# Moving the last columns' scores and values, and beginning the up matmuls with half contractions, in a fused pooling-attention and gated feed-forward kernel

One Trainium2 chip, one core. The metric is device time in microseconds (us); lower is better. The kernel before takes 303.98 us (median of 3 runs, 303.52 to 304.59).

## The reference

Keys and values of 8 batches x 8 heads (576 tokens, 64 per head) are averaged over groups of 8 tokens, then plain attention, then a feed-forward block with the gate h cos(h):

```python
k_p = k.reshape(B, H, Sp, 8, D).mean(axis=3)          # Sp = 72
v_p = v.reshape(B, H, Sp, 8, D).mean(axis=3)
attn = softmax(q @ k_p^T / sqrt(D))
x = (attn @ v_p).transpose(0, 2, 1, 3).reshape(4608, 512)
h = x @ w_in                                          # 512 -> 2048
out = (h * np.cos(h)) @ w_out                         # 2048 -> 512
```

## The kernel before

The feed-forward runs over nine tiles of 512 tokens (loop variable t). A batch has 576 tokens, so batch b begins 64 b tokens behind tile b. While the down matmuls of tile t run, a list `fill` slips the attention of batch b = t + 1 in among them; each entry is (number of the down matmul ahead of which it is issued, what). A batch is cut into units: u0, u1 (columns 0 to 255, heads 0-3 and 4-7), u2, u3 (columns 256 to 511), and REST (the last 64 columns, all heads). REST of batch t is left for pass t. "Vn" is the values unit of un.

```python
SEG = ((0, 256), (256, 256), (512, 64))
REST = (SEG[2], (0, H))
BY_TOKENS = [(SEG[s], (4 * j, 4)) for s in range(2) for j in range(2)]
...
banks = [psum.tile([128, 2, 512], FP32, name=f"bank{i}") for i in range(3)]
obanks = [psum.tile([128, 512], FP32, name=f"obank{i}") for i in range(2)]
...
def values(b, u, pair, later=None):            # matmuls, 2 logarithms + 1 exponential (ScalarE) ...
    ...
    def mul():                                 # ... and 2 multiplications (VectorE) that write xT
        for hp in range(2):
            nc.vector.tensor_mul(out=x_out(b, u, half[hp]), in0=cols(pair[half[hp], hp, :], u), in1=...)
    if later is None:
        mul()
    else:
        later.append(mul)
...
def up_mm(t, fp, k0=0, k1=KCH):                # a pair of 128-wide chunks; KCH = 4 steps of contraction
    h = banks[fp % 3]
    for j in range(2):
        fc = 2 * fp + j
        for ki in range(k0, k1):               # ki covers heads 2 ki and 2 ki + 1
            nc.tensor.matmul(h[:, j, :], lhsT=w_in_sb[fc // 4][:, ki, ...],
                             rhs=xT[:, ki, t * TILE:(t + 1) * TILE], start=(ki == 0), stop=(ki == KCH - 1))
...
for t in range(NT):
    b = t + 1
    for fp in range(FFCH // 2):                # the up stage: 64 matmuls
        up_mm(t, fp, 2 if t == 0 and fp < 2 else 0)
        ...
        up_g(t, fp, between)                   # cosine (ScalarE), multiplication (VectorE), frees the bank
    ...
    for n, (ms, fc) in enumerate(mms):         # the down stage: 64 matmuls, with fill among them
        while fi < len(fill) and fill[fi][0] <= n:
            fill[fi][1]()
            fi += 1
        down_mm(obanks[ms % 2], ms, fc)
        if fc == FFCH - 1:
            down_out(t, ms, obanks[ms % 2])    # VectorE copies the bank out, then a DMA
```

The softmax here doesn't subtract the row's maximum and nothing guards it: scores larger than these inputs give would overflow.

## Time and profile before

| | before |
|---|---|
| time, us (median of the first 3 runs) | 303.98 |
| span in the profile, us | 302.1 |
| TensorE busy | 97%, full clock |
| one pass, up stage to up stage, t = 1 to 6 | 31.40 to 31.41 us each |

The prediction shows the lines themselves. In them, a row of the order of time has start, length, engine, line, operation, tiles, shapes and count; L297 is an up matmul, L310 a down matmul, L211 scores, L241 values, L252 the multiplication into xT, L316 the copy of a finished down bank, PEld the weight loads. A row of waits has who waited, for what, the total in us, how many times, and the longest; "issue" means that the profile shows nothing that was waited for. Groups overlap at their edges because a matmul is recorded longer (0.38 us) than its slot (0.216 us); so I read starts, not lengths. A gap below is the distance from one matmul's start to the next one's; a hole is what a gap has over its usual value. Pair fp is the pair of 128-wide chunks 2 fp and 2 fp + 1 of the up stage; pair 3 takes the bank that pair 0 has left.

### The profile page before, as it was taken

The numbers are of one execution on the slowest core, as the hardware profiler recorded it, in microseconds if no ns is written. First come the engines' busy times: TensorE is split into PE (matmuls) and PEld (weight loads), VectorE is DVE, ScalarE is ACT, GpSimd is POOL, SyncE is SP. The second block draws the span as 40 slices with busy tenths as digits, with TensorE's granted clock in tenths as the row PEclk, the third lists the DMA queues.
The fourth block names the chain that finished last, engine by engine and source line by source line (L and its number), as shares of the span: only waits on it lengthen the run. The fifth ranks groups of instructions, "written<-read, shape, count | busy, mean of one in ns | idle before, by whom it ended". The sixth has DMA issues, their size and how long they took to land.

```text
span 302.1 us, 4605 instructions
## 1 busy us (share of the span) xinstructions
PE 294.0 (97%) x1798; PEld 141.6 (47%) x1798; DVE 172.3 (57%) x211; ACT 206.8 (68%) x255; POOL 129.8 (43%) x92
## 2 busy tenths in 40 slices
PE   8799999999999999999999999999999999999995
PEld 3545544445544454455444544454444544444444
DVE  5558636574566366645675566656574567425712
ACT  3887897469856986688768876788578956606500
POOL 8553007984973596349733991399100000000000
PEclk9999999999999999999999999999999999999999
DMA  7999999639546943695169617881900330131032
GB/s 152 201 207 206 208 204 196 152 44 174 109 113 105 167 92 70 123 171 113 44 132 161 115 36 162 129 141 36 167 5 1 71 69 0 27 79 35 0 71 71
DMA packets 44006, 32.92 MB, mean 109 GB/s; under 512 B 22096, under 2 KB 39248, under 8 KB 43984
## 3 DMA queue, kind: packets, MB, share of 16 engines
q0 software_dynamic: 19744, 18.07, 38.2%
q1 hardware_dynamic: 24080, 14.42, 21.0%
q8 instruction: 14, 0.23, 0.3%
q10 hardware_dynamic: 160, 0.13, 0.2%
q14 instruction: 8, 0.07, 0.1%
HBM read 36.70 MB, written 9.44 MB: 153 GB/s over the span
## 4 chain that ended last, share of the span: by engine, by line
PE 85%; DMA 10%; POOL 2%; ACT 1%; issue 0%; DVE 0%; POOLq 0%; ACTq 0%
PE obank L310 39%; PE bank L297 37%; DMA w_out_sb<-in_moe_w_out_dram 6%; PE bank L241 5%; DMA w_in_sb<-in_moe_w_in_dram 4%; PE bank L211 3%; PE bank L328 1%; POOL kv_st L84 1%; POOL kp L384 1%; POOL q_b L84 1%; ACT L285 0%; ACT cos L304 0%; ACT ex L218 0%; POOL identity masks.py:197 0%; DVE o_sb L316 0%
## 5 line engine op out<-in xcount | busy, mean ns | idle before, releaser
L310 PE MATMUL obank<-w_out_sb,g_sb 128*128 128x512 bf16 x560 | 132.5, 380 | 0.5 <-DMA w_out_sb<-in_moe_w_out_dram 0.5
L297 PE MATMUL bank<-xT,w_in_sb 128*128 128x512 bf16 x576 | 126.5, 379 | 0.0
L304 ACT ACTIVATE cos<-bank,half_pi 128x1024 f32<-128x1024 f32 x72 | 80.0, 1113 | 63.3 <-PE bank L297 63.3
L307 DVE TENSOR_TENSOR g_sb<-bank,cos 128x1024 bf16<-128x1024 f32 x72 | 88.1, 1225 | 48.2 <-ACT cos L304 48.2
L297 PEld LDWEIGHTS <-w_in_sb 128*128 128x128 bf16 x576 | 55.5, 98 | 68.6 <-DVE xT L252 2.5
L310 PEld LDWEIGHTS <-g_sb 128*128 128x128 bf16 x560 | 52.2, 97 | 56.9 <-issue 3.7
L252 DVE TENSOR_TENSOR xT<-bank,inv 64x512 bf16<-64x512 f32 (+1 forms) x72 | 45.3, 629 | 50.1 <-ACT inv L248 49.2
L141 POOL TENSOR_TENSOR kv_st<-kv_st 72x2048 f32<-72x2048 bf16 x12 | 48.7, 4056 | 35.2 <-DMA kv_st<-in_k_dram 35.2
L247 ACT ACTIVATE lnc<-bank 64x512 f32<-64x512 f32 (+1 forms) x72 | 39.2, 544 | 2.9 <-PE bank L241 1.3
L218 ACT ACTIVATE ex<-bank 72x1024 bf16<-72x1024 f32 (+1 forms) x40 | 35.0, 928 | 5.3 <-PE bank L211 5.2
L316 DVE COPY o_sb<-obank 128x512 f32<-128x512 f32 x35 | 23.6, 689 | 16.8 <-PE obank L310 16.2
L142 POOL TENSOR_TENSOR kv_st<-kv_st 72x1024 f32<-72x1024 f32 x12 | 28.2, 2348 | 1.0
L248 ACT ACTIVATE inv<-lnc 128x512 f32<-128x512 f32 (+1 forms) x36 | 21.0, 583 | 1.1
L241 PE MATMUL bank<-ex,vz 72*128 72x256 bf16 (+1 forms) x176 | 20.0, 243 | 0.2 <-ACT ex L218 0.2
L241 PEld LDWEIGHTS <-vz 72*128 72x128 bf16 x176 | 13.7, 97 | 9.9 <-issue 0.6
L145 POOL TENSOR_TENSOR kp<-kv_st 72x512 bf16<-72x512 f32 x12 | 14.9, 1264 | 0.5
L211 PE MATMUL bank<-qT,kk 64*72 64x256 bf16 (+1 forms) x192 | 13.3, 252 | 1.1 <-ACT qT L193 0.5
L211 PEld LDWEIGHTS <-kk 64*72 64x72 bf16 x192 | 7.6, 110 | 11.9 <-issue 8.1
L285 ACT ACT_TABLE_LOAD x9 | 11.5, 1283 | 0.9 <-PEq L515 0.7
L288 ACT ACT_TABLE_LOAD x9 | 11.5, 1283 | 0.2
L495 POOL COPY gate<-kk 1x1 bf16<-1x1 bf16 x5 | 0.9, 180 | 24.7 <-DMA kk<-kp 24.7
L84 POOL DMA_DIRECT2D q_b<-in_q_dram x10 | 7.7, 773 | 2.7 <-DMA w_in_sb<-in_moe_w_in_dram 1.4
(55 smaller groups left out, 89.8 us busy)
## 6 DMA issues: line engine op xcount, KB each, us to landing
out_dram<-o_sb SPq DMA_DIRECT2D x70, 128.0 KB, 2.4
kv_st<-in_v_dram POOLq DMA_DIRECT2D x8, 576.0 KB, 13.0
kv_st<-in_k_dram POOLq DMA_DIRECT2D x7, 576.0 KB, 7.7
q_b<-in_q_dram POOLq DMA_DIRECT2D x6, 576.0 KB, 9.9
w_in_sb<-in_moe_w_in_dram POOLq DMA_DIRECT2D x4, 512.0 KB, 13.7
w_out_sb<-in_moe_w_out_dram POOLq DMA_DIRECT2D x4, 512.0 KB, 18.4
q_b<-in_q_dram POOLq DMA_DIRECT2D x4, 288.0 KB, 12.1
g_sb<-in_k_dram SPq DMA_DIRECT2D x1, 576.0 KB, 3.5
```

The lines of the kernel that those rows point to most:

```text
L141: add(out=s, in0=x[:, :, 0:4, :], in1=x[:, :, 4:8, :], op=ADD)
L142: add(out=s[:, :, 0:2, :], in0=s[:, :, 0:2, :], in1=s[:, :, 2:4, :], op=ADD)
L211: nc.tensor.matmul(pair[:Sp, bank, c:c + n].rearrange("p (g n) -> p g n", n=64), lhsT=kk[b % 2][half[r], h0 + i, 0:Sp], rhs=att["qT", b][h ...
L218: nc.scalar.activation(out=ex[:, 0:nh * n].rearrange("p (a n) -> p a n", a=2), in_=pair[:Sp, :, 0:nh * n // 2], func=ACTF.Exp, scale=scale ...
L241: nc.tensor.matmul(pair[:, hp, (i // 2) * n:(i // 2 + 1) * n], lhsT=vz[b % 2][:, pj, 2 * hp:2 * hp + 2, :].rearrange("p a d -> p (a d)"), ...
L247: nc.scalar.activation(out=lnc[half[1 - hp]], in_=pair[half[1 - hp], hp, 0:w], func=ACTF.Ln)
L252: nc.vector.tensor_mul(out=x_out(b, u, half[hp]), in0=cols(pair[half[hp], hp, :], u), in1=cols(inv[half[1 - hp]], u))
L297: nc.tensor.matmul(h[:, j, :], lhsT=w_in_sb[fc // 4][:, ki, (fc % 4) * 128:(fc % 4 + 1) * 128], rhs=xT[:, ki, t * TILE:(t + 1) * TILE], st ...
L304: nc.scalar.activation(out=cos, in_=h, func=ACTF.Sin, bias=half_pi[:, :1])
L307: nc.vector.tensor_mul(out=g_sb[:, 2 * fp:2 * fp + 2, :], in0=h, in1=cos)
L310: nc.tensor.matmul(o, lhsT=g_sb[:, fc, ms * 128:(ms + 1) * 128], rhs=w_out_sb[fc // 4][:, fc % 4, :], start=(fc == 0), stop=(fc == FFCH - 1))
L316: nc.vector.tensor_copy(out=o[:, 0:n], in_=ps)
```

## The change

The intent: go to the 64-row mode of the scores once less per pass (REST's scores right behind u2's and u3's); let REST's values come ahead of the last unit V3; and, because V3 is then late, begin the next up stage with matmuls that need heads 0 to 3 alone. V0's multiplication is issued behind the first output copy (list `later`).

```diff
     for t in range(NT):
         b = t + 1
+        if t > 0:
+            up_mm(t, 0, 0, 2)
+            up_mm(t, 1, 0, 2)
         for fp in range(FFCH // 2):
-            up_mm(t, fp, 2 if t == 0 and fp < 2 else 0)
+            up_mm(t, fp, 2 if fp < 2 else 0)
...
-            late = 0 < t and b < B
-            fill = [(1, lambda: scores(t, REST, banks[2])), (12, lambda: values(t, REST, banks[2 if late else 1]))]
+            fill = [(1, lambda: scores(t, REST, banks[2])), (12, lambda: values(t, REST, banks[1]))]
...
-            def two_(n, bank0, bank1):
+            def scores_of(*parts):
                 def go():
-                    for mm in (scores_mm, scores_exp):
-                        mm(b, us[n], banks[bank0])
-                        mm(b, us[n + 1], banks[bank1])
+                    for f in scores_mm, scores_exp:
+                        for b_, u, bank in parts:
+                            f(b_, u, banks[bank])
                 return go
-            fill = [(4, two_(0, 2, 0)), (14, V_(0, 1)), (19, V_(1, 2)), (32, two_(2, 0, 1)), (36, fill[0][1]),
-                    (38, V_(2, 0)), (41, V_(3, 1)), (45, fill[1][1])]
+            fill = [(4, scores_of((b, us[0], 2), (b, us[1], 0))), (14, V_(0, 1, later)), (16, lambda: later.pop()()),
+                    (19, V_(1, 2)), (35, scores_of((b, us[2], 0), (b, us[3], 1), (t, REST, 2))),
+                    (38, V_(2, 0)), (43, lambda: values(t, REST, banks[1])), (46, V_(3, 2))]
```

## The prediction

> **What bounds the kernel now.** I read the page first (busy shares, clock, chain), then the stretches of the main loop, then the waits of TensorE and of its weight loads, and last the order of time in one pass of the loop.
>
> ```profile
> span 302.1 us, 4605 instructions
> PE 294.0 (97%) x1798; PEld 141.6 (47%) x1798; DVE 172.3 (57%) x211; ACT 206.8 (68%) x255; POOL 129.8 (43%) x92
> ...
> PEclk9999999999999999999999999999999999999999
> ...
> PE 85%; DMA 10%; POOL 2%; ACT 1%; issue 0%; DVE 0%; POOLq 0%; ACTq 0%
> ```
>
> TensorE is busy 97% of the span at the full clock, and the chain that ended last is TensorE for 85%. Busy alone does not prove a full TensorE, so I take the pace from starts. In the up stage of the second loop pass, 64 matmuls take 13.81 us on the chain (53.66 to 67.47): 0.2158 us each. That is the pace of a stream without a hole. The stretches from one up stage to the next:
>
> ```profile
> core 0: us, PE busy (x) PEld busy (x) DVE busy (x) ACT busy (x) POOL busy (x), PEclk, DMA share, GB/s
> 53.66:84.98 31.32, 31.32 (x178) 14.87 (x176) 18.33 (x22) 24.14 (x30) 25.81 (x16) 1.00 0.63 115
> 84.98:116.39 31.41, 31.41 (x178) 14.89 (x178) 18.82 (x23) 24.23 (x31) 21.14 (x12) 1.00 0.64 115
> 116.39:147.80 31.41, 31.41 (x178) 14.88 (x178) 18.82 (x23) 24.23 (x31) 19.21 (x12) 1.00 0.64 115
> ```
>
> Each of the six passes t = 1 to 6 takes 31.4 us, alike to 0.1. The 128 large matmuls need 128 x 0.2158 = 27.62; 3.8 us are left for scores, values and what is lost at their edges. Only holes in those edges are to be won. The weight loads show where they are (stretch 60 to 260 us, six passes):
>
> ```profile
> PEld L211 <- issue: 5.5, 13, 0.4
> PEld L211 <- DVE xT L252: 2.5, 6, 0.4
> PEld L297 <- DVE xT L252: 2.5, 6, 0.4
> PEld L310 <- issue: 2.3, 12, 0.2
> ```
>
> Six times a weight load of the up stage (L297) and six times one of the scores (L211) is held by VectorE's write of xT. These idle times are of the weight-load row and lie mostly under the matmul that still runs, so they are not the loss. The loss comes from the starts of TensorE's groups in one pass (start, length, line, count):
>
> ```profile
> 107.27 0.63 PE L211 MATMUL bank<-qT,kk 64*72 64x256 bf16 x8
> 107.83 1.04 PE L310 MATMUL obank<-w_out_sb,g_sb 128*128 128x512 bf16 x4
> 108.80 0.33 PE L211 MATMUL bank<-qT,kk 64*72 64x64 bf16 x8
> 109.06 0.60 PE L310 MATMUL obank<-w_out_sb,g_sb 128*128 128x512 bf16 x2
> ...
> 112.13 4.27 PE L310 MATMUL obank<-w_out_sb,g_sb 128*128 128x512 bf16 x19
> 116.31 0.82 PE L297 MATMUL bank<-xT,w_in_sb 128*128 128x512 bf16 x3
> ```
>
> The last 19 down matmuls take 116.31 - 112.13 = 4.18 us from first start to the first up matmul; at pace they need 4.10. So **the hole ahead of an up stage is 0.08 us**. The group of the last 64 columns (L211, 64x64) sits between down matmuls: from 107.83 to 109.06 are 1.23 us for four down matmuls (0.86) and this group, so it costs 0.37, though its 8 matmuls run in four pairs about 0.033 us apart (0.13, single starts in the trace).
>
> **What the Trainium skill says.** (1) "TensorE: Matmul & The Clock Gate", section "Back-to-back issue gap", gives about 216 ns for 512 columns at full clock as N/2.4 + 2.5, and says that a real stream can sustain 131. This trace agrees with the first (215.8) and not with the second: the pace can't fall below it here. (2) "TensorEngine Tiling (Array Packing)", "Key Properties", says that a change of tiling mode drains TensorE. Scores contract over 64 rows, everything around them over 128 or 72, so each visit is two changes; the trace agrees: four down matmuls ahead of a scores group take 0.97 (107.83 to 108.80) for 0.86, and 0.13 of the 0.26 behind it is not its pairs. (3) The same TensorE page, "Architectural detail: the array is 16× 32×32, not 1× 128×128", has ScalarE and VectorE strictly first in, first out. The trace agrees on VectorE below: an output copy stands between two multiplications that were issued around it. (4) "Perfetto Trace Analysis", "Identifying the Most-Contended Engine", warns that matmul busy is no measure of what is left; that is why I use starts.
>
> **The change, part by part.**
>
> *1. Last columns' scores behind the second score group (six passes).* It removes one visit to the 64-row mode: 0.37 becomes 0.13, which would save 0.24. But it needs bank 2, which the second values unit (V1) has to leave. VectorE and ScalarE in that pass:
>
> ```profile
> 105.19 1.39 DVE L252 TENSOR_TENSOR xT<-bank,inv 64x512 bf16<-64x512 f32 x2 [3.90 <-ACT inv L248]
> 106.61 0.69 DVE L316 COPY o_sb<-obank 128x512 f32<-128x512 f32 x1
> 107.33 1.39 DVE L252 TENSOR_TENSOR xT<-bank,inv 64x512 bf16<-64x512 f32 x2
> ...
> 106.42 0.63 ACT L248 ACTIVATE inv<-lnc 128x512 f32<-128x512 f32 x1
> 107.72 2.41 ACT L218 ACTIVATE ex<-bank 72x1024 bf16<-72x1024 f32 x3 [0.68 <-PE bank L211]
> ```
>
> The change delays V0's multiplication behind the copy, so that the copy runs early (its bank is full at about 103.5) and V1's multiplication starts when its reciprocal is there: 106.42 + 0.63 + 0.03 = 107.08, ends 108.47 instead of 108.72. The joint group starts three down matmuls later than now, at 107.27 + 0.65 = 107.92; its first four pairs, 0.108 apart, end their issue at 108.35. The last columns then want bank 2 and get it at 108.47 + 0.08 = 108.55 (0.08 is what the trace shows from 108.72 to the weight load at 108.80). So **a new hole of 0.20 opens inside the group**. With the 0.26 of the small group the next down matmul (number 35) starts at 108.81 and number 36 at 109.03; today number 36 starts at 109.06. What is left of 0.24 is 0.03.
>
> *2. The exponentials come later.* First exponential: 0.45 behind the group's start (today 107.72 - 107.27), so 108.37 to 109.39 at 1.02. V2 would be issued at 109.03 + 2 x 0.216 = 109.46 and needs it at 109.39 + 0.06 = 109.45: just in time. The third exponential ends near 110.85 (2.41 after 108.37, with slack); the last columns' values, five down matmuls behind V2, come at 109.46 + 0.44 + 1.08 = 110.98: in time. ScalarE is then 0.65 later than today: V2's logarithms and reciprocal, 110.85 to 112.7; the last columns', to 114.0; V3's, to 115.85; table load (1.28) to 117.15. No hole on TensorE from any of them.
>
> *3. V3 last, and half contractions first.* The two half groups need heads 0 to 3 only (V0, V2 and the last columns, written by about 115.1) and banks 0 and 1. The up stage begins near 116.2, so it waits for nothing: **0.08 saved, in the up stages t = 2 to 7**. V3's multiplication runs 115.87 to 117.27 on VectorE; the second halves start 8 x 0.216 = 1.73 after the beginning, 117.95: 0.7 to spare.
>
> *4. The price of halves.* Pair 0 is now complete after 12 matmuls, not 8. Its cosine starts 1.94 after the beginning today (118.25 - 116.31), so 2.80 then; cosine 1.11, multiplication 1.23 and 0.03 between: bank 0 is free at 5.17, seen by TensorE at 5.23. Pair 3 wants it at 24 x 0.216 = 5.18. So **0.04 to 0.05 is lost in every up stage t = 1 to 8**. The kernel has this pattern already at t = 0, where the start of pair 3 is 250 ns behind its predecessor instead of 216: 0.035 measured. I take 0.04.
>
> Sum: 6 x 0.08 (begin) + 6 x 0.03 (scores) - 8 x 0.04 (pair 3) = 0.48 + 0.18 - 0.32 = 0.34 us less. Other engines' work is the same in kind and count. 303.98 - 0.34 = 303.64; I round down to 303.5 because where I chose between two values I took the worse.
>
> **Rivals.** *A: the joint group does not wait for bank 2*, or the wait covers the drain. Then 0.24 instead of 0.03 in six passes, 1.3 us more: about 302.4. For it: dependences may be by part of the bank, so that the first multiplication (0.7 earlier) lets most through. Against: the pairs go to both halves, and today's weight load there does wait for xT. Even then V2 would wait for the first exponential (109.45), which eats most of the gain. *B: the later ScalarE chain becomes the bound*: V3's multiplication is 0.7 later than I have it, or V2 stalls 0.1 to 0.2 on its exponential; six passes of 0.2 give 1.2 us, about 304.8. For it: V2 and the last columns' values have hardly any slack. Against: V3 has 0.7, and a stall at V2 pushes all else back with it. *C: pair 3's wait doubles* (0.09 as at the beginning of an up stage): 8 x 0.05 more, 304.0. *D: DMA or the clock*: nothing in the loop's chain, and the clock is at 9 in all slices; no effect.
>
> **Range and chances.** All terms are hundredths of a us, taken six or eight times; the worst sums that I can build are -2 and +1.5 us. The three runs before spread over 1.1 us. Two per cent are 6.1 us, and all edges of six passes (3.8 us each, most of it needed work) hold nothing like it. Range 302.5 to 304.3; within 2% nearly sure.
>
> **What would show it.** In the changed trace: the pass (up stage to up stage) 31.41 becomes 31.3 to 31.4; the weight load of L297 no longer waits for xT at the beginning; one scores visit less per pass, with 24 matmuls in one group, and inside it a wait of about 0.2 on VectorE's xT; the output copy near 103.6; V2 within 0.05 of its exponential's end; a hole near 0.04 ahead of pair 3. Wrong it would be if the second halves wait for V3's multiplication, if V2 stalls by 0.1 or more, or if the joint group runs through and the pass falls to 31.1.

## The result, and the profile after

303.33 us (median of 4 runs, 303.28 to 303.87) against 303.75 (4 runs of before, 303.52 to 304.59): 0.42 us less. The ratio is 0.9985, 95% interval 0.9962 to 1.0009: same within 2%, and by the times alone not told from no change. (A ratio here is the mean time of one kernel's runs over that of the other's of the same rounds, so not quite the ratio of the medians.) Executions over 1.5% slower than the fastest of the same kernel are left out of the means. The traces are much finer than the times, because the passes repeat. The stretches from up stage to up stage of the kernel after, with the columns as in the prediction:

```profile
core 0: us, PE busy (x) PEld busy (x) DVE busy (x) ACT busy (x) POOL busy (x), PEclk, DMA share, GB/s
53.53:84.83 31.30, 31.30 (x177) 15.07 (x176) 17.25 (x20) 23.38 (x30) 25.76 (x15) 1.00 0.62 115
84.83:116.12 31.29, 31.29 (x177) 15.05 (x176) 18.72 (x23) 24.14 (x31) 19.84 (x12) 1.00 0.63 115
```

A pass is 31.29 to 31.30 us instead of 31.41. What held the weight loads, 60 to 260 us, after:

```profile
PEld L211 <- issue: 5.5, 13, 0.4
PEld L211 <- DVE xT L252: 1.5, 6, 0.2
PEld L310 <- issue: 1.2, 6, 0.2
PEld L297 <- issue: 0.9, 6, 0.2
```

The up stage's wait for xT is gone. L310's edge count halves (12 to 6): one visit to the scores' mode less per pass. Scores still wait for xT, now inside the joint group; and L297 has a new small idle ("issue", 0.9 in six), which is pair 3. TensorE's order of time in the third pass, and VectorE's:

```profile
107.71 0.93 PE L211 MATMUL bank<-qT,kk 64*72 64x256 bf16 x16
108.57 0.82 PE L310 MATMUL obank<-w_out_sb,g_sb 128*128 128x512 bf16 x3
109.23 0.60 PE L241 MATMUL bank<-ex,vz 72*128 72x256 bf16 x4
...
112.07 4.05 PE L310 MATMUL obank<-w_out_sb,g_sb 128*128 128x512 bf16 x18
115.95 1.24 PE L297 MATMUL bank<-xT,w_in_sb 128*128 128x512 bf16 x5
```

```profile
103.27 0.69 DVE L316 COPY o_sb<-obank 128x512 f32<-128x512 f32 x1 [2.20 <-PE obank L310]
104.98 1.39 DVE L252 TENSOR_TENSOR xT<-bank,inv 64x512 bf16<-64x512 f32 x2 [1.01 <-ACT inv L248]
106.87 1.39 DVE L252 TENSOR_TENSOR xT<-bank,inv 64x512 bf16<-64x512 f32 x2 [0.50 <-ACT inv L248]
...
115.63 1.39 DVE L252 TENSOR_TENSOR xT<-bank,inv 64x512 bf16<-64x512 f32 x2 [0.86 <-ACT inv L248]
```

18 down matmuls from 112.07 to the first up matmul at 115.95 take 3.88, which is 18 x 0.2158: no hole. The joint group takes 108.57 - 107.71 = 0.86. V1's multiplication ends at 106.87 + 1.39 = 108.26, inside the group. From the single starts of matmuls in the trace (their gaps, not a duration): ahead of the first REST score the gap is 245 ns where its neighbours have 106, a **hole of 139 ns**; ahead of pair 3 of the up stage it is 249 instead of 216, a **hole of 33 ns**. V3's multiplication ends at 117.02, 1.07 us after the up stage began.

From the first up matmul of pass t = 1 to the start of the last matmul, the trace of before has 244.57 us and that of after 243.93: 0.64 us less in the loop. The part ahead of it has unchanged code; it ends at 53.50 us before and 53.36 after, and anywhere from 53.28 to 53.80 in nine of the ten traces. From the last matmul's start to the end of the span, before has 4.03 us and after 4.21: 0.19 more. Together this makes the 0.6 by which the spans differ; the medians differ by 0.42.

### The profile page after: what moved, and what is told of

Read it like the earlier page. It is cut to its first block, busy times and chain, and to the rows that moved or that the text cites. A ratio compares the mean times of both kernels' runs of the same rounds, so it can differ in the third digit from the quotient of the medians.

```text
span 301.5 us, 4599 instructions
## 1 busy us (share of the span) xinstructions
PE 292.7 (97%) x1798; PEld 142.2 (47%) x1798; DVE 171.4 (57%) x211; ACT 206.1 (68%) x255; POOL 129.7 (43%) x92
## 4 chain that ended last, share of the span: by engine, by line
PE 92%; DMA 2%; ACT 2%; issue 1%; POOL 1%; DVE 1%; POOLq 0%; ACTq 0%; DVEq 0%
PE bank L297 41%; PE obank L310 40%; PE bank L241 5%; PE bank L211 3%; DMA q_b<-in_q_dram 2%; PE bank L328 1%; ACT ex L218 1%; PE obank L157 0%; ACT L285 0%; PE obank L192 0%; ACT cos L304 0%; PE bank L165 0%; PE obank L280 0%; POOL q_b L84 0%; POOL kv_st L84 0%
## 5 line engine op out<-in xcount | busy, mean ns | idle before, releaser
L310 PE MATMUL obank<-w_out_sb,g_sb 128*128 128x512 bf16 x560 | 131.4, 379 | 0.0
L297 PE MATMUL bank<-xT,w_in_sb 128*128 128x512 bf16 x576 | 126.6, 379 | 0.0
L297 PEld LDWEIGHTS <-w_in_sb 128*128 128x128 bf16 x576 | 56.1, 98 | 67.6 <-issue 1.6
L310 PEld LDWEIGHTS <-g_sb 128*128 128x128 bf16 x560 | 52.8, 98 | 56.5 <-issue 1.9
```

The lines of the kernel that those rows point to most:

```text
L297: nc.tensor.matmul(h[:, j, :], lhsT=w_in_sb[fc // 4][:, ki, (fc % 4) * 128:(fc % 4 + 1) * 128], rhs=xT[:, ki, t * TILE:(t + 1) * TILE], st ...
L310: nc.tensor.matmul(o, lhsT=g_sb[:, fc, ms * 128:(ms + 1) * 128], rhs=w_out_sb[fc // 4][:, fc % 4, :], start=(fc == 0), stop=(fc == FFCH - 1))
```

## The experiments

All were correct. A few executions of before, e1, e3, e10, e11 and e12 had a mean granted clock of 0.98 to 0.99 and took 3 to 5 us more; all but one (e1's 308.96) were counted, and they blur the ratios (stated below). One of them was profiled, e10's (306.69 us, mean clock 0.989): its granted clock was 0.78 from 10 to 20 us and 0.88 from 20 to 30 us, and 1.00 in the other stretches that were read; its up stage t = 1 begins at 56.96 us, over 3 us later than in the other traces, and its passes are not longer: nearly all of what it lost lies ahead of the loop. I therefore also give medians of the executions with a clock of 0.99 or more, and the lengths of passes in the profiled run, which repeat to 12 ns within a run. In the second call, on another chip than the first, the change itself was run again as a control.

| run | pass, us | loop from up stage t = 1 to the last start, us | median at clock 0.99 or more, us |
|---|---|---|---|
| before | 31.41 | 244.57 | 303.60 (6, first), 303.75 (11, second) |
| the change | 31.295 | 243.93 | 303.33 (4) |
| e1 halves only | 31.46 | 244.91 | 303.99, 304.35 (2) |
| e2 order only | 31.27 (four), 31.96 (two) | 245.10 | 304.60 (4) |
| e3 group at 36 | 31.13 | 242.95 | 302.65 (3) |
| e6 V0 not delayed | 31.56 | 245.52 | 304.55 (4) |
| e5 REST's scores apart | 31.35 | 244.28 | 303.77 (1) |
| e10 halves at t = 2, 3 | 31.26 (four), 31.29 (two) | 243.73 | 303.12 (5) |
| e11 both | 31.095 (four), 31.13 (two) | 242.73 | 302.15 (4) |
| e12 the change again | 31.295 | 243.93 | 303.32 (5) |

My theory was the sum of the prediction. The rivals were that the halves, or the order, or the delay do nothing or everything alone.

### e1: the halves alone

```diff
 # on the kernel before
+        if t > 0:
+            up_mm(t, 0, 0, 2)
+            up_mm(t, 1, 0, 2)
-            up_mm(t, fp, 2 if t == 0 and fp < 2 else 0)
+            up_mm(t, fp, 2 if fp < 2 else 0)
```

> Only the half contractions, in the order of before (last columns' values last, scores apart). My theory: halves alone win nothing, because the last columns' multiplication writes all of xT and still ends last, so the 0.09 us hole ahead of each up stage stays, and pair 3 waits 0.033 in each of eight up stages. Pass 31.41 + 0.03 = 31.44 us, total about 0.3 us over before. Rival (the halves themselves bring the gain, by giving VectorE 1.7 us more): the hole goes and the pass is near 31.33 to 31.35.

Measured: pass 31.458, loop 0.34 us longer than before; the ratio of the rounds is 1.0032 (0.9944 to 1.012). Waits of the weight loads:

```profile
PEld L297 <- DVE xT L252: 2.5, 6, 0.4
PEld L310 <- issue: 2.3, 12, 0.2
PEld L297 <- issue: 0.9, 6, 0.2
```

The wait for xT is exactly as before (2.5 in six) and pair 3's has come on top. By itself this part is a loss; the rival falls.

### e2: the order alone

```diff
 # on the changed kernel
-        if t > 0:
-            up_mm(t, 0, 0, 2)
-            up_mm(t, 1, 0, 2)
-            up_mm(t, fp, 2 if fp < 2 else 0)
+            up_mm(t, fp, 2 if t == 0 and fp < 2 else 0)
```

> Only the new order of scores and values, whole contractions. My theory: V3's multiplication ends 1.07 us after the up stage begins, and the third matmul of the stage wants it 0.43 after it; 0.7 us stall in six passes, less the 0.033 at pair 3. Pass 31.295 + 0.67 = 31.96, total 4.0 us over after, 3.4 over before (about 307). Rival (the order is the gain and the halves only insurance): pass at or under 31.30.

Measured: two passes of 31.956, as I had computed for all six, and four of 31.273. Median 304.60, ratio of the rounds 1.0008 (0.9939 to 1.0076). I expected about 307: **a miss**, by 2.4 us. TensorE and VectorE at the beginning of the up stage t = 3, and of t = 5, in this run:

```profile
117.03 0.59 PE L297 MATMUL bank<-xT,w_in_sb 128*128 128x512 bf16 x2
118.15 3.18 PE L297 MATMUL bank<-xT,w_in_sb 128*128 128x512 bf16 x14 [0.52 <-DVE xT L252]
```

```profile
116.70 1.39 DVE L252 TENSOR_TENSOR xT<-bank,inv 64x512 bf16<-64x512 f32 x2 [0.86 <-ACT inv L248]
```

```profile
180.26 2.11 PE L297 MATMUL bank<-xT,w_in_sb 128*128 128x512 bf16 x9
```

```profile
179.93 1.39 DVE L252 TENSOR_TENSOR xT<-bank,inv 64x512 bf16<-64x512 f32 x2 [0.86 <-ACT inv L248]
```

At t = 3 the third matmul waits until V3's multiplication ends (116.70 + 1.39 = 118.09). At t = 5 the multiplication is as late against the up stage (it ends at 181.32, the third matmul starts at about 180.69), yet nothing waits. The reason is in the indices: V3 writes columns 256 to 511 of batch b, tokens 576 b + 256 and on; tile b ends at 512 b + 512. They overlap only while 64 b < 256, that is b up to 3. I had treated all passes alike because they looked alike. So the halves are needed at t = 2 and 3 alone (ahead of up stage t = 1 the attention of batch 1 had another schedule, and it does not stall here either), and elsewhere they should only cost pair 3's hole. e10 tests that.

### e3: the joint group one down matmul later

```diff
-  (35, scores_of((b, us[2], 0), (b, us[3], 1), (t, REST, 2))),
-  (38, V_(2, 0)), (43, lambda: values(t, REST, banks[1])), (46, V_(3, 2))]
+  (36, scores_of((b, us[2], 0), (b, us[3], 1), (t, REST, 2))),
+  (40, V_(2, 0)), (45, lambda: values(t, REST, banks[1])), (48, V_(3, 2))]
```

> The change with the joint scores group one down matmul later (36), V2 at 40, last columns' values at 45, V3 at 48. My theory: the 137 ns hole inside the joint group is the wait for V1's multiplication to leave bank 2 and is covered by one down matmul of 216 ns; nothing else waits (V2 1.6 us behind the group for an exponential that needs 1.5; V3's multiplication has 0.25 us to spare). Pass 31.295 - 0.137 = 31.16, total 0.8 us under after. Rival 1 (the hole is the price of going from 256-column to 64-column scores in one group): it stays, pass 31.30. Rival 2 (it comes back as a stall at V2 or at the second halves): pass 31.25 to 31.30 with the hole moved there.

Measured: pass 31.130, 0.165 under the change; loop 0.98 us under it; median 302.65; ratio of the rounds 0.9971 (0.9896 to 1.0046, with a run at clock 0.982 in it). TensorE in the third pass:

```profile
108.11 0.76 PE L211 MATMUL bank<-qT,kk 64*72 64x256 bf16 x16
108.81 1.04 PE L310 MATMUL obank<-w_out_sb,g_sb 128*128 128x512 bf16 x4
109.68 0.60 PE L241 MATMUL bank<-ex,vz 72*128 72x256 bf16 x4
```

The group takes 108.81 - 108.11 = 0.70 instead of 0.86, and V2 follows four down matmuls later without a hole (109.68 - 108.81 = 0.87). The gap ahead of the first REST score is 106 ns like its neighbours (139 less), and the next one 25 instead of 52 (27 less): together the 0.165 of the pass. So the hole was the wait for bank 2, not a price of the shapes (rival 1), and it did not come back elsewhere (rival 2).

### e6: V0's multiplication at once

```diff
-  (14, V_(0, 1, later)), (16, lambda: later.pop()()),
+  (14, V_(0, 1)),
```

> The change, but V0's multiplication issued at once, so that the first output copy stands behind it on VectorE again. My theory: V1's multiplication starts behind the copy, 0.25 us later, and the hole in the joint group grows from 137 to about 390 ns; pass 31.295 + 0.25 = 31.55, total 1.5 us over after, so slower than before. Rival (the delay is cosmetic, slack absorbs it): pass 31.30.

Measured: pass 31.558 (expected 31.55), median 304.55, ratio of the rounds 1.001 (0.9952 to 1.0068). VectorE:

```profile
105.55 1.39 DVE L252 TENSOR_TENSOR xT<-bank,inv 64x512 bf16<-64x512 f32 x2 [3.90 <-ACT inv L248]
106.97 0.69 DVE L316 COPY o_sb<-obank 128x512 f32<-128x512 f32 x1
107.69 1.39 DVE L252 TENSOR_TENSOR xT<-bank,inv 64x512 bf16<-64x512 f32 x2
```

The copy stands in line behind V0's multiplication again, as in the kernel before. The size is right but the place only in part: the hole in the joint group grew from 139 to about 220 ns, not to 390; the other 182 ns stand ahead of down matmul 32 (a gap of 398), which reuses the bank that this copy empties at 107.66. Before, the score group stood at 32 and covered that; with the group at 35 nothing does. So the delay pays twice, and without it the whole change would be a loss.

### e5: REST's scores apart

```diff
-  (35, scores_of((b, us[2], 0), (b, us[3], 1), (t, REST, 2))),
+  (32, scores_of((b, us[2], 0), (b, us[3], 1))), (36, fill[0][1]),
```

> The change with the last columns' scores apart again (second score group at 32, last columns' scores at 36), all else as changed. My theory: the visit costs 0.37 apart and 0.13 plus a hole of 0.137 joined, and the hole ahead of the up stage stays away; so the pass is 31.41 - 0.09 + 0.03 = 31.35, 0.06 above the change, about 0.35 us over six passes. Rival (the joining itself brings nothing, the order of the values is all): 31.30 as in the change.

Measured: pass 31.353, 303.77 in its single run (state unknown). No gap in its passes shows a wait on VectorE: all three score groups begin with the same 309 ns. Joining is worth 31.353 - 31.295 = 0.058 in the change; without the wait (e3) it would be 31.353 - 31.130 = 0.223. The wait took three quarters of it.

### e10, e11 and e12: halves only where needed; both improvements; the change again

```diff
+        halves = t in (2, 3)
-        if t > 0:
+        if halves:
             up_mm(t, 0, 0, 2)
             up_mm(t, 1, 0, 2)
-            up_mm(t, fp, 2 if fp < 2 else 0)
+            up_mm(t, fp, 2 if (halves or t == 0) and fp < 2 else 0)
```

e11 is this with e3's `fill`; e12 is the change as it is.

> The change with half contractions only in the up stages t = 2 and 3. The order-only run stalled in these two alone: the units of columns 256 to 511 of a batch lie in the next tile of tokens only for the first three batches. My theory: the other six up stages need no halves and lose 0.02 to 0.035 each at pair 3 by them; their up stages fall from 13.845 to 13.813 us, passes without halves to 31.27, total 0.15 to 0.2 us under the change. Rival (the halves do something in all stages, such as shielding a late bank): stalls appear in stages 4 to 8, total over the change.

> Both improvements: the joint group at 36 (V2 40, last columns 45, V3 48) and halves only at t = 2 and 3. My theory: passes 31.13 with halves and 31.10 without, total 1.1 to 1.3 us under the change, near 302.2, with an interval wholly under 1 against before. Rival: one of the gains is given back where the later V3 meets whole contractions (passes above 31.13).

> The change itself once more, unchanged, for its size beside the others on one chip: 0.4 to 0.6 us under before (ratio near 0.998), passes 31.295. Rival: noise, passes the same as before.

Measured: e10 has passes of 31.26 and two of 31.29, loop 0.20 us under the change, no stall in any up stage from t = 1 on. e12 repeats the change's passes to 5 ns (31.293 to 31.298), median 303.32 against 303.75 of before. e11 is the fastest: up stages on its chain, start, length and line,

```profile
84.60 13.85 PE bank L297 x64
115.72 13.85 PE bank L297 x64
146.85 13.81 PE bank L297 x64
177.95 13.81 PE bank L297 x64
```

13.85 with halves and 13.81 without: pair 3's price is 0.03 per stage (0.032 by the passes, 31.127 against 31.095). e11's loop is 1.2 us under the change and 1.84 under before; its four full-clock runs have 302.05 to 302.26 against 302.84 to 303.98 for the eleven of before. The ratios that the rounds gave (e10 1.0005, 0.9972 to 1.0038; e11 0.9988, 0.9948 to 1.0028; e12 1.0012, 0.9981 to 1.0042) contain one, two and one executions at a clock of 0.983 to 0.989, and none of before; I expected e11's interval wholly under 1 and did not get it, most likely because of its two slow executions. By the medians of full-clock runs, e11 is 1.6 us, half a per cent, under before.

## Why the prediction was right

The direction was right, and so were the mechanisms, but for the claim that all six up stages need the halves. The sum was not: the loop gained 0.64 where 0.34 was worked out, mostly by term 2. That 303.33 came so close to 303.5 is partly luck. The end of the program took 0.19 back, for which the prediction had no term; the figure had been rounded down by 0.14; and it was counted from 303.98, where four runs of before gave 303.75. The range (302.5 to 304.3) holds the time of before too, so the total alone tells little; the passes and the holes decide.

1. *The hole ahead of the up stage* (0.08 each, six times): gone in the trace after, there again in e1, which kept the order. By single starts it was 0.09 (gaps of 296 and 226 for 216 each): 0.54 us in all.
2. *Joining the scores* (0.24 less a hole of 0.20, leaving 0.03, six times): this is the term that was mis-sized. The joining alone is worth 0.223 (e5 against e3), close to 0.24; the wait costs 0.165 in all (e3 against the change), not 0.20; 0.058 is left, twice my figure, 0.35 us in all. Two small errors made it: I took 0.08 from VectorE's end to the weight load out of the trace before, but there the mode change alone would have put the load at the same place (the gap is 309 ns, as ahead of the score groups that wait for nothing; in e5 VectorE had ended 0.33 ahead of the load and the gap was 309 all the same); after, it is 0.05 (108.26 to 108.31). And four pairs of scores take 0.46, not 0.43, until the next could start.
3. *The later exponentials*: V2 was issued at 109.23 with its exponential ready at about 109.2, as tight as computed; its gap is 220 ns instead of 216. The joint group has 16 matmuls (8 and 8, in eight pairs), not the 24 that the prediction names; its sums use the pairs and are not touched by that.
4. *Halves make room for V3*: V3's multiplication ends 1.07 us after the beginning, the second halves start at 1.73. There is room in all passes, but it is needed in two only; the prediction spoke as if all six needed it, which e2 refuted. It cost the forecast nothing, since the halves were there in all.
5. *Pair 3* (0.04, eight times): 0.033 in the trace, shown by removal in e10 and e11 (six stages without halves: 0.20 us in e10); 0.26 us in all.

Sum as measured: 0.54 + 0.35 - 0.26 = 0.63 us, and the loop is 0.64 shorter. Predicted were 0.48 + 0.18 - 0.32 = 0.34. Of the rivals, A (no wait at bank 2) is what e3 brought about; in the change itself the wait was there. B (a later ScalarE chain as the bound) and C (a doubled wait at pair 3) did not show. D held for the change: its four executions had a clock of 0.999 or 1.000. Single executions with a lower clock occur in before as well.

The medians differ by 0.42 where the loops differ by 0.64, and by the traces the end of the program accounts for nearly all of that (0.64 - 0.19 = 0.45). From the last matmul's start to the end of the span, before, e1 and e6 take 4.00 to 4.03 us, and the other seven traces 4.21 to 4.22, both of the change among them. VectorE's last DRAIN instruction starts 3.52 us after that matmul in before and 3.86 in after, and what follows it comes 0.19 later. Why this is so in some kernels and not in others, whose last stage has the same code, was not tested and stays open.

## What to carry to other kernels

When one engine is full, a reordering is worth only the gaps between the starts on that engine, so sum them from single starts before and expect no more. A saved switch is paid back by whatever buffer the moved work now meets earlier: look up when that buffer comes free, and move the group by one step (here one matmul later gave 1 us). And before guarding every iteration against a late producer, check by the indices which iterations read it at all.

## What the Trainium skill lacked or had wrong

- "TensorE: Matmul & The Clock Gate", "Back-to-back issue gap", gives 131 ns as the sustained spacing for 512 columns in a real stream of weight loads and matmuls. Here the mean over an up stage at full clock never went under 215.8 ns (64 in 13.81 us), in all ten kernels; its other figure, about 216, which it gives for an isolated matmul, is the one that fits this stream.
- "TensorEngine Tiling (Array Packing)", "Key Properties", says that a mode change drains TensorE but gives no cost. Here a down matmul ahead of a 64-row group is followed after 309 ns instead of 216, and the last 256-column pair of such a group is followed after about 200 instead of 106: 93 ns in and 95 ns out. One visit less, with nothing waiting, saved 223 ns (e5 against e3).
- No page has the time from a VectorE result to the TensorE instruction that waits for it: 51 to 53 ns here, in each of the six waits inside the joint group of the change's trace (as from 108.26 to 108.31).
